# Copies and sums out of PSUM, split by bank, and an order that knows of the banks

## The chip, the cores and the metric

The kernel runs on one core of a Trainium2 chip. The metric is the device time of one execution in microseconds. Three timed runs of the kernel before gave 785.96, 789.14 and 790.19 us; the median, 789.14 us, is the time to compare with. A profiled execution of the same kernel had a span of 774.2 us from its first to its last instruction, with a granted TensorE clock of 0.997.

## The reference

Two blocks follow each other. The first is a linear recurrence over 768 positions, for 4 batches and 8 heads of width 40. The second sends each of the 3072 resulting rows (320 wide) to one of 8 experts, an expert being two matrix products with a ReLU between them.

```python
# r, k, v, w, a, b: (4, 8, 768, 40)
state = np.zeros((B, H, D, D), dtype=np.float32)
for t in range(S):
    kt, vt, rt = (k[:, :, t], v[:, :, t], r[:, :, t])
    wt, at, bt = (w[:, :, t], a[:, :, t], b[:, :, t])
    y[:, :, t] = np.einsum('bhd,bhde->bhe', rt, state)
    Sa = np.einsum('bhde,bhe->bhd', state, at)
    state_decay = state * wt[:, :, None, :] - np.einsum('bhd,bhe->bhde', Sa, bt)
    state = state_decay + np.einsum('bhd,bhe->bhde', vt, kt)

x = y.transpose(0, 2, 1, 3).reshape(B * S, H * D)          # (3072, 320)
logits = x @ w_gate                                        # 8 experts
expert_idx = np.argmax(logits, axis=1)
# gate_w: the softmax weight of the chosen expert
# for each expert e, over its rows:
h = np.maximum(x_sorted[lo:hi] @ w1[e], 0.0)               # w1[e]: 320 x 1024
y_sorted[lo:hi] = h @ w2[e]                                # w2[e]: 1024 x 320
# back in the order of the rows, times gate_w
```

## The kernel before

The recurrence is done in chunks of 64 positions. A **unit** is one chunk of half the batches; there are 24 (12 chunks, 2 halves). Inside a unit the effect of the 64 positions on each other is the inverse of a triangular matrix, which is built by repeated squaring: `X` holds a power, its transpose and a running sum, and three rounds double the power. Each round multiplies on TensorE into PSUM, and ScalarE and VectorE bring the products back to SBUF.

PSUM is one tile of 8 banks. A matmul group takes one bank or an even pair of them. In a pair the first index of the data (`q`, 0 or 1) is the bank, so bank 0 holds one half of the heads and bank 1 the other.

```python
psum = pp.tile([128, 8, 512], F32, name="ps")
def pair(h, width, w=0):                    # a pair of banks: x, bank, p, d
    return psum[:, h.at : h.at + 2, w * NP * C : w * NP * C + NP * width].rearrange("x a (p d) -> x a p d", p=NP)
def copy(e, dst, src):
    if e == ACT:
        nc.scalar.copy(dst, src)            # L494
    else:
        nc.vector.tensor_copy(dst, src)     # L496
def mm(out_, lhsT, rhs, start=True, stop=True):
    nc.tensor.matmul(...)                   # L499
```

Every operation of the recurrence is a `Step`: a rank, an engine (`ANY` is ScalarE or VectorE), a cost in us by the program's own model, a function that emits the instructions, and the `Held` objects that it reads and writes. `Held` stands for a piece of a buffer or for PSUM banks. Before anything is emitted, `in_order` walks over the steps that are ready, gives each a start on its engine, takes the one that can start first (the rank decides among equals) and emits it. The order of the instructions on each engine is the outcome. The semaphores that keep the engines apart are put in afterwards, by what each instruction reads and writes. For PSUM that is done by bank: two instructions of different engines on one bank follow each other in the order in which they were emitted, also where both only read.

```python
def when(s):
    return {e: max((d.done - (d.lag if d.on == e and e != SP else 0.0) for d in s.deps), default=0.0)
            for e in ((ACT, DVE) if s.eng == ANY else (s.eng,))}
# ...
for s, r in ready.items():
    new = [h for h in s.ps if h.at is None]
    for e in r:
        t0 = max(r[e], free[e])
        ask = t0 + (WAIT if s.eng == ANY and e == DVE else 0.0)     # WAIT = 1.00
        # ... free banks, cost
        key = (ask, s.rank[0] + uneven, s.rank, t0 + cost)
```

The model above lets two engines read one bank at a time.

The groups of matmuls whose result is read by two engines:

```python
# 1. N and GT out of one pair (p_a); the mask of GT is applied by GpSimd
Step(rk - 1.3, DVE, 0.69, ... nc.vector.tensor_tensor(d, s(), m, op=ALU.mult), reads=[ps], writes=held)      # N, L583
Step(rk - 2.0, ACT, 0.59, ... nc.scalar.copy(d, s()), reads=[ps], writes=held)                               # GT, L585
# 2. T and the first sums out of ONE bank (N transposed)
for i, (z, par) in enumerate(((0, 0), (1, 1), (0, 1), (1, 0))):
    Step(rk - 0.1, ANY, 0.36, ... copy(e, T1[halves[z], :, par, :], ...), reads=[ps], writes=hT1[i : i + 1])
Step(rk - 0.5, DVE, 1.38, first_sums, reads=[ps], writes=hX[2:3])                                            # L607
# 3. three squarings: new power, new transpose and new sum
def sums(e, dst, src, old):
    nc.vector.tensor_tensor(dst[:, 0], src[:, 0], old[:, 0], op=ALU.add)                                     # L620
    for h in range(2):
        o_ = halves[1 - h]
        nc.vector.tensor_tensor(dst[o_, 1], src[o_, 1], old[halves[h], 1], op=ALU.add)                       # L623
while 8 * k <= C:
    # a pair for the power: 16 matmuls, one copy
    Step(rk, PE, 4 * ROUND, ... p_power(e, pair(ps, C), X, 1, 0), reads=hX[:2], writes=[ps], n=64)
    Step(rk - 0.9, ANY, 0.59, ... copy(e, Xn[:, :, :, 0, :], pair(ps, C)), reads=[ps], writes=hXn[0:1])
    # a pair that holds both the transpose and the sum
    Step(rk, PE, 0.81, ... p_sum(e, half_sums(ps, 2), X, 2), reads=hX, writes=[ps], n=64)
    Step(rk, ANY, 0.59, ... copy(e, Xn[:, :, :, 1, :], half_sums(ps, 2)[:, :, :, 0, :]), reads=[ps], writes=hXn[1:2])
    Step(rk, DVE, 1.29, ... sums(e, Xn[:, :, :, 2, :], half_sums(ps, 2)[:, :, :, 1, :], X[:, :, :, 2, :]),
         reads=[ps] + hX[2:3], writes=hXn[2:3])
    X, hX = Xn, hXn
    k *= 2
# 4. M and TT out of the last pair
Step(rk, DVE, 0.69, ... nc.vector.tensor_tensor(M[:], half_sums(ps, 2)[:, :, :, 0, :], eye(2, NP), op=ALU.add), ...)   # M, L673
def kept(e, ps=ps, TT=TT):
    src = half_sums(ps, 2)[:, :, :, 1, :]
    copy(e, TT[:, 0], src[:, 0])
    for h in range(2):
        copy(e, TT[halves[h], 1], src[halves[1 - h], 1])
Step(rk + 0.1, ANY, 1.1, kept, reads=[ps], writes=hTT)
Step(rk - 1.0, POOL, 1.22, ... nc.gpsimd.tensor_tensor(TT[:], TT[:], X[:, :, :, 2, :], op=ALU.add), ...)               # L683
```

Further on a unit turns v and k (`nV`, `nKB`), adds the state (`rhs`, `W`, `Vu`, `ZU`), writes y and the new state, and computes the logits and the scaled rows `xs`. The first expert's work begins inside the same order; the others follow outside it.

Of the kernel before, what the change touches and what calls it, by code (L numbers as in the profile page):

```python
# [15 lines left out]
ALU = mybir.AluOpType  # L16
# [7 lines left out]
def kernel(  # L24
# [245 lines left out]

    class Step:
        def __init__(self, rank, eng, cost, fn, reads=(), writes=(), after=(), lag=0.2, n=0, shape=None, first=-1):
            self.rank, self.eng, self.cost, self.fn, self.lag, self.n = (rank, len(steps)), eng, cost, fn, lag, n
            self.shape, self.first = shape, shape if first == -1 else first
# [19 lines left out]
    def in_order():  # L294
# [13 lines left out]

        def place(new, t):

            ok = [f is not None and f <= t for f in bank_free]
            at = []
            for h in new:
                n = h.banks
                b = next((b for b in (range(7, -1, -1) if n == 1 else range(0, 8, 2)) if all(ok[b : b + n])), None)
                if b is None:
                    return None
                ok[b : b + n] = [False] * n
                at.append(b)
            return at  # L320
# [10 lines left out]
        while ready:  # L331
            times = sorted({f for f in bank_free if f is not None})
            best = None
            for s, r in ready.items():
                new = [h for h in s.ps if h.at is None]
                for e in r:
                    t0 = max(r[e], free[e])
# [45 lines left out]
            free[e] = end  # L383
            s.on, s.done = e, end + s.lag
            s.fn(e)
# [17 lines left out]
    with tc.tile_pool(name="ring", bufs=1) as ring, \  # L403
# [4 lines left out]
        class Ring:  # L408
# [19 lines left out]
        r_GT = Ring("GT", [NP, 2, C], 1)  # L428
        r_N = Ring("N", [NP, 2, C], 1)
        r_X = Ring("X", [2, NP, 3, C], 0)  # L430
        r_X.bufs = [
            (wx[:, i * XN : (i + 1) * XN].rearrange("x (q p w j) -> x q p w j", q=2, p=NP, w=3), [Held() for _ in range(3)]) for i in range(XB)
        ]
        r_M = Ring("M", [2, NP, C], 2)
        r_TT = Ring("TT", [2, NP, C], 2)
# [41 lines left out]
        for i, (name, cost, part) in enumerate(first_constants()):  # L477
            step = Step(-98.5 if name else -60 + i + 0.3, POOL, cost, lambda e, part=part: part(), writes=[h_ones] if name else [], lag=0.2)
            if not name:
                basis.append(step)  # L480
# [29 lines left out]
        def unit(u):  # L510
# [37 lines left out]
            Step(pre, DVE, 1.4, lambda e: nc.vector.tensor_tensor_scan(  # L548
# [3 lines left out]
            Step(pre, DVE, 0.2, lambda e: nc.vector.reciprocal(qi[:, :, 0], r3[:, :, 1]), reads=hrv, writes=hqi)  # L552
            Step(pre, ACT, 0.25, lambda e: nc.scalar.copy(pc[:], r3[:, :, 1]), reads=hrv, writes=hpc)
            Step(pre + 1.0, DVE, 1.3, lambda e: nc.vector.tensor_tensor_scan(  # L554
                qq[:], dec[:, : SEG * C1], qi[:].rearrange("p s j -> p (s j)"), 0.0, op0=ALU.mult, op1=ALU.add,
            ), reads=hdec + hqi, writes=hq)
            for q in range(2):
                kb = KB[:, :, q]
                by = behind[:, q * NP : (q + 1) * NP].unsqueeze(2).to_broadcast([128, NP, 2, C])
                Step(pre - 0.1, POOL, 1.2, lambda e, kb=kb, by=by: nc.gpsimd.tensor_tensor(kb, kb, by, op=ALU.mult),  # L560
                     reads=hrv + hKB[2:], writes=hKB[q : q + 1])
            Step(pre, POOL, 1.22, lambda e: nc.gpsimd.tensor_tensor(Aq[:], Aq[:], q3[:, :, :C], op=ALU.mult), reads=hq, writes=hA)  # L562
# [12 lines left out]
            Step(rk - 1.0, PE, 0.81, p_a, reads=hKB + hA, writes=[ps], n=64)  # L575
            for t, held, i, mask, by in ((N1, hN1, 1, m_neg, DVE), (GT, hGT, 0, m_low, ACT)):
# [5 lines left out]
                if by == DVE:  # L582
                    Step(rk - 1.3, DVE, 0.69, lambda e, d=dst_, s=src_, m=mask: nc.vector.tensor_tensor(d, s(), m, op=ALU.mult), reads=[ps], writes=held)  # L583
                else:
                    Step(rk - 2.0, ACT, 0.59, lambda e, d=dst_, s=src_: nc.scalar.copy(d, s()), reads=[ps], writes=held)  # L585
                    Step(rk, POOL, 1.2, lambda e, d=dst_, m=mask: nc.gpsimd.tensor_tensor(d, d, m, op=ALU.mult), writes=held)  # L586
# [11 lines left out]
            Step(rk - 0.6, PE, 0.47, by_blocks(N1, ps), reads=hN1, writes=[ps], n=8, shape=WHOLE)  # L598
            blocks = lambda ps=ps: psum[:, ps.at, :].rearrange("x (p z j) -> x p z j", p=NP, z=2)
            for i, (z, par) in enumerate(((0, 0), (1, 1), (0, 1), (1, 0))):  # L600
                Step(rk - 0.1, ANY, 0.36, lambda e, z=z, par=par, blocks=blocks: copy(e, T1[halves[z], :, par, :], blocks()[halves[par], :, z, :]),
                     reads=[ps], writes=hT1[i : i + 1])
# [8 lines left out]
            Step(rk - 0.5, DVE, 1.38, first_sums, reads=[ps], writes=hX[2:3])  # L611
            Gk, hGk = r_Gk.take()
            ps = Held(1)
            Step(rk - 0.6, PE, 0.47, by_blocks(GT, ps), reads=hGT, writes=[ps], n=8, shape=WHOLE)
            Step(rk + 1.0, ANY, 0.59, lambda e, ps=ps: copy(e, Gk[:].rearrange("x p z j -> x (p z j)"), psum[:, ps.at, :]), reads=[ps], writes=hGk)
# [3 lines left out]
            def sums(e, dst, src, old):  # L619
                nc.vector.tensor_tensor(dst[:, 0], src[:, 0], old[:, 0], op=ALU.add)  # L620
                for h in range(2):
                    o_ = halves[1 - h]
                    nc.vector.tensor_tensor(dst[o_, 1], src[o_, 1], old[halves[h], 1], op=ALU.add)  # L623
# [9 lines left out]
            for i in range(2):  # L633
                Step(rk, ANY, 0.59, lambda e, i=i, ps=ps, X=X: copy(e, X[:, :, :, i, :], pair(ps, C, i)), reads=[ps], writes=hX[i : i + 1])
# [17 lines left out]
            while 8 * k <= C:  # L652
# [3 lines left out]
                Step(rk, PE, 4 * ROUND, lambda e, ps=ps, X=X: p_power(e, pair(ps, C), X, 1, 0), reads=hX[:2], writes=[ps], n=64)  # L656
                Step(rk - 0.9, ANY, 0.59, lambda e, ps=ps, Xn=Xn: copy(e, Xn[:, :, :, 0, :], pair(ps, C)), reads=[ps], writes=hXn[0:1])
                ps = Held(2)
                Step(rk, PE, 0.81, lambda e, ps=ps, X=X: p_sum(e, half_sums(ps, 2), X, 2), reads=hX, writes=[ps], n=64)
                Step(rk, ANY, 0.59, lambda e, ps=ps, Xn=Xn: copy(e, Xn[:, :, :, 1, :], half_sums(ps, 2)[:, :, :, 0, :]),  # L660
                     reads=[ps], writes=hXn[1:2])
                Step(rk, DVE, 1.29, lambda e, ps=ps, X=X, Xn=Xn: sums(
                    e, Xn[:, :, :, 2, :], half_sums(ps, 2)[:, :, :, 1, :], X[:, :, :, 2, :],
                ), reads=[ps] + hX[2:3], writes=hXn[2:3])
# [6 lines left out]
            Step(rk, PE, 0.81, lambda e, ps=ps, X=X: p_sum(e, half_sums(ps, 2), X, 2), reads=hX, writes=[ps], n=64)  # L671

            Step(rk, DVE, 0.69, lambda e, ps=ps, M=M: nc.vector.tensor_tensor(  # L673
                M[:], half_sums(ps, 2)[:, :, :, 0, :], eye(2, NP), op=ALU.add,
            ), reads=[ps], writes=hM)

            def kept(e, ps=ps, TT=TT):
                src = half_sums(ps, 2)[:, :, :, 1, :]
                copy(e, TT[:, 0], src[:, 0])
                for h in range(2):  # L680
                    copy(e, TT[halves[h], 1], src[halves[1 - h], 1])
            Step(rk + 0.1, ANY, 1.1, kept, reads=[ps], writes=hTT)
            Step(rk - 1.0, POOL, 1.22, lambda e, X=X, TT=TT: nc.gpsimd.tensor_tensor(TT[:], TT[:], X[:, :, :, 2, :], op=ALU.add), reads=hX[2:3], writes=hTT)  # L683

# [5 lines left out]
            Step(rk - 0.1, ANY, 0.59, lambda e, ps=ps: copy(e, nV[:].rearrange("x p a d -> x (p a d)"), psum[:, ps.at, :]), reads=[ps], writes=hnV)  # L690
# [11 lines left out]
            for i in range(2):  # L702
                Step(rk + 0.4, ANY, 0.59, lambda e, i=i, ps=ps: copy(
                    e, nKB[:, i * NP : (i + 1) * NP].rearrange("x b a d -> x (b a d)"), psum[:, ps.at + i, :],
                ), reads=[ps], writes=hnKB[i : i + 1])
# [25 lines left out]
            Step(rk - 0.1, PE, 8 * ROUND if c else 4 * ROUND, p_rhs, reads=hGk + hnV + (hST + hA if c else []), writes=[ps], n=128 if c else 64)  # L731
# [6 lines left out]
            Step(rk + 3.7, ANY, 0.85, to_rhs, reads=[ps], writes=hrhs)  # L738
# [9 lines left out]
            Step(rk + 0.7, PE, 4 * ROUND, p_w, reads=hM + hrhs, writes=[ps], n=64)  # L748
            Step(rk + 0.3, ANY, 0.42, lambda e, ps=ps: copy(e, W[:, :, :, :D], pair(ps, D)), reads=[ps], writes=hW)
            if c:  # L750
                ps = Held(1)
                Step(rk, PE, 0.47, by_blocks(ST, ps), reads=hST, writes=[ps], n=8, shape=WHOLE)
                Step(rk, ANY, 0.42, lambda e, ps=ps: copy(
# [13 lines left out]
            Step(rk + 0.1, PE, 4 * ROUND, p_uT, reads=hTT + hW, writes=[ps], n=64)  # L767
# [22 lines left out]
            for s in range(2):  # L790
                Step(rk + 0.5, DVE, 0.69, lambda e, s=s, ps=ps: nc.vector.tensor_tensor(
                    ZU[:, s, :, :C], psum[:, ps.at + s, :].rearrange("x (b j) -> x b j", j=C),
                    m_plus[:, None, :].to_broadcast([128, SEG, C]), op=ALU.mult,
                ), reads=[ps], writes=hZU[s : s + 1])
            if not last:
                ps = Held(2)
                Step(rk + 0.3, PE, 0.92, turned(lambda p, par: Vu[:, p, 2 * par : 2 * par + 2], ps), reads=hV + huT, writes=[ps], n=16, shape=WHOLE)
                for i in range(2):
# [3 lines left out]
                    Step(rk + 0.4, ANY, 0.42, uv, reads=[ps], writes=hZU[2 + i : 3 + i])  # L802
# [14 lines left out]
            Step(rk + 0.4, PE, (0.57 if c else 0) + 0.48 + 0.96 * w / 104, p_y, reads=hnKB + (hZU[:2] if last else hZU) + (hSn + hR if c else []), writes=[psy], n=128 if c else 64, shape=TALL, first=None if c else TALL)  # L817
# [22 lines left out]
            Step(late, PE, 1.0, p_x, reads=hxT + [h_tg], writes=[psx], n=16, shape=WHOLE)  # L840
# [10 lines left out]
            Step(late + 0.6, DVE, 0.4, logits, reads=[psx], writes=[hl])  # L851
            Step(late + 0.3, ACT, 0.5, lambda e: nc.scalar.activation(
# [468 lines left out]
```

## Time and profile before

| what | value |
|---|---|
| median of three runs | 789.14 us |
| span of the profiled execution | 774.2 us |
| ScalarE: 128x512 copies into wx | 192 of 590 ns |
| VectorE: sums of a squaring, L620 (128x256) and L623 (64x256) | 72 and 144 of 422 ns |
| VectorE: first sums, L607 (64x512) | 48 of 688 ns |
| GpSimd: GT's mask, L586 | 24 of 1310 ns |
| DMA | 61.06 MB, mean 79 GB/s |

How to read it: PE is TensorE's matmul row and PEld its weight-load row, DVE is VectorE, ACT ScalarE, POOL GpSimd. Lines such as L494 are lines of the kernel; because every copy goes through one helper, the tile names (`wx<-ps`) tell the operations apart. `wx` is the buffer of the powers `X`. Two stages are seen in the span: the recurrence to about 505 us, with many small matmuls (64 x 64), and the experts after it, with few large ones.

### The profile page before, as it was taken

What the parts mean: (1) busy time and instruction counts of PE and PEld (TensorE: products, weight loads), DVE (VectorE), ACT (ScalarE), POOL (GpSimd) and SP (SyncE); (2) the same over time, 40 slices, a digit from 0 to 9 for tenths busy, and PEclk for the clock granted to TensorE, in tenths of its full rate; (3) what the DMA queues carried; (4) which work ended last, traced back from release to release, by engine and by line L of the source; (5) the groups of instructions that cost most, each with busy time, mean ns of one, the idle gap of its engine ahead of it and who ended that gap; (6) DMA issues with size and microseconds to landing.
All of it is one profiled execution on the core that took longest, in us unless ns stands there. A gap on an engine that the chain in (4) does not pass through costs nothing. (4 is left out here: it accounts for less than half of the span.)

```text
span 774.2 us, 35470 instructions
## 1 busy us (share of the span) xinstructions
PE 715.5 (92%) x15712; PEld 554.2 (72%) x15712; DVE 371.9 (48%) x804; ACT 346.9 (45%) x840; POOL 291.8 (38%) x472
## 2 busy tenths in 40 slices
PE   3988999999998998999999898799999999999995
PEld 2877888888877887888988888665656565564653
DVE  7667666667666666667576666640201112010110
ACT  2665766566665665666757666421101111111010
POOL 8742145723653366334852470313413110111101
PEclk9999999999999999999999999999999999999998
DMA  4332223323212321232232211333953126002000
GB/s 96 87 79 56 66 59 72 98 53 93 64 40 70 81 68 41 71 97 74 65 77 71 52 31 41 112 92 117 330 161 130 51 78 207 23 16 84 24 0 28
DMA packets 120368, 61.06 MB, mean 79 GB/s; under 512 B 100688, under 2 KB 116051, under 8 KB 120212
## 3 DMA queue, kind: packets, MB, share of 16 engines
q1 hardware_dynamic: 112776, 46.20, 22.5%
q0 software_dynamic: 3136, 9.44, 3.7%
q10 hardware_dynamic: 4300, 3.12, 1.4%
q8 instruction: 124, 2.03, 1.1%
q14 instruction: 32, 0.26, 0.1%
HBM read 50.08 MB, written 9.31 MB: 77 GB/s over the span
## 5 line engine op out<-in xcount | busy, mean ns | idle before, releaser
L499 PE MATMUL ps<-wx 64*64 64x128 f32 (+1 forms) x5376 | 147.4, 251 | 11.6 <-ACT wx L494 7.6
L494 ACT COPY wx<-ps 128x512 f32<-128x512 f32 (+1 forms) x196 | 110.8, 587 | 79.1 <-PE ps L499 42.6
L499 PEld LDWEIGHTS ps<-wx 64*64 64x64 f32 x5376 | 124.2, 134 | 25.4 <-ACT wx L494 10.8
L1160 DVE TENSOR_SCALAR h_sb<-hp 128x448 f32<-128x448 f32 (+1 forms) x32 | 18.4, 574 | 189.1 <-PE hp L1155 162.6
L247 POOL DMA_INDIRECT out_dram<-zo,s_idx x21 | 20.8, 989 | 150.2 <-ACT zo L1177 149.6
L1171 PE MATMUL zp<-w,h_sb 128*128 128x320 f32 (+1 forms) x272 | 71.0, 433 | 0.0
L560 POOL TENSOR_TENSOR KB<-KB,rv 128x512 f32<-128x512 f32 x48 | 58.3, 1235 | 18.0 <-DMA KB<-in_packed_dram 5.7
L623 DVE TENSOR_TENSOR wx<-ps,wx 64x256 f32<-64x256 f32 x144 | 60.8, 422 | 3.0
L1161 ACT ACTIVATE h_sb<-hp 128x448 f32<-128x448 f32 (+1 forms) x32 | 16.1, 504 | 101.2 <-PE hp L1155 52.0
L1171 PEld LDWEIGHTS zp<-w,h_sb 128*128 128x128 f32 (+1 forms) x272 | 44.4, 174 | 20.5 <-issue 1.3
L1177 ACT COPY zo<-zp 128x320 f32<-128x320 f32 x25 | 10.7, 426 | 104.9 <-PE zp L1171 104.9
L562 POOL TENSOR_TENSOR A<-A,q 128x512 f32<-128x512 f32 x24 | 28.4, 1185 | 72.9 <-DVE q L554 55.0
L620 DVE TENSOR_TENSOR wx<-ps,wx 128x256 f32<-128x256 f32 x72 | 30.4, 422 | 53.1 <-ACT wx L494 32.5
L586 POOL TENSOR_TENSOR GT<-GT,m_low 128x512 f32<-128x512 f32 x24 | 31.4, 1310 | 61.6 <-ACT GT L585 61.6
L683 POOL TENSOR_TENSOR TT<-TT,wx 128x512 f32<-128x512 f32 x24 | 30.8, 1281 | 62.4 <-ACT TT L494 61.8
L1171 PE MATMUL zp<-wx,h_sb 128*128 128x320 f32 (+1 forms) x192 | 53.0, 433 | 0.0
L1147 PE MATMUL hp<-xgT,w 128*128 128x448 f32 x128 | 51.1, 547 | 0.0
L494 ACT COPY T<-ps 64x256 f32<-64x256 f32 x94 | 34.5, 367 | 35.6 <-DVE wx L607 29.3
L1171 PEld LDWEIGHTS zp<-wx,h_sb 128*128 128x128 f32 (+1 forms) x192 | 33.4, 177 | 13.2 <-issue 0.8
L1147 PEld LDWEIGHTS hp<-xgT,w 128*128 128x128 f32 x128 | 23.5, 190 | 25.8 <-issue 25.5
L499 PE MATMUL ps<-ZU,nKB 128*64 128x104 f32 (+1 forms) x768 | 38.8, 253 | 0.1
L607 DVE TENSOR_TENSOR wx<-ps,ihalf 64x512 f32<-64x512 f32 x48 | 33.0, 688 | 8.1 <-ACT T L494 2.1
(246 smaller groups left out, 1362.2 us busy)
## 6 DMA issues: line engine op xcount, KB each, us to landing
KB<-in_packed_dram SPq DMA_DIRECT2D x188, 40.0 KB
w<-in_moe_w_dram SPq DMA_DIRECT2D x16, 320.0 KB
x_rows<-xs SPq DMA_DIRECT2D x24, 192.0 KB
w<-in_moe_w_dram SPq DMA_DIRECT2D x8, 512.0 KB
dec<-in_packed_dram SPq DMA_DIRECT2D x96, 40.0 KB
Vu<-in_packed_dram SPq DMA_DIRECT2D x96, 40.0 KB
wx<-in_moe_w_dram SPq DMA_DIRECT2D x12, 320.0 KB
A<-in_packed_dram SPq DMA_DIRECT2D x92, 40.0 KB
```

Of the source, the lines that this page charges most:

```text
L247: ins_ = nc.gpsimd.indirect_dma_start(out=out[:, :], out_offset=bass.IndirectOffsetOnAxis(ap=si, axis=0), in_=zo, in_offset=None, bounds_c ...
L494: nc.scalar.copy(dst, src)
L499: nc.tensor.matmul(out_, lhsT=lhsT, rhs=rhs, start=start, stop=stop, skip_group_check=True)
L560: Step(pre - 0.1, POOL, 1.2, lambda e, kb=kb, by=by: nc.gpsimd.tensor_tensor(kb, kb, by, op=ALU.mult), reads=hrv + hKB[2:], writes=hKB[q : ...
L562: Step(pre, POOL, 1.22, lambda e: nc.gpsimd.tensor_tensor(Aq[:], Aq[:], q3[:, :, :C], op=ALU.mult), reads=hq, writes=hA)
L586: Step(rk, POOL, 1.2, lambda e, d=dst_, m=mask: nc.gpsimd.tensor_tensor(d, d, m, op=ALU.mult), writes=held)
L607: nc.vector.tensor_tensor(for_q[:, :, ::-1] if par else for_q, blocks()[halves[par]], ihalf[halves[par], None, None, :].to_broadcast([HP, ...
L620: nc.vector.tensor_tensor(dst[:, 0], src[:, 0], old[:, 0], op=ALU.add)
L623: nc.vector.tensor_tensor(dst[o_, 1], src[o_, 1], old[halves[h], 1], op=ALU.add)
L683: Step(rk - 1.0, POOL, 1.22, lambda e, X=X, TT=TT: nc.gpsimd.tensor_tensor(TT[:], TT[:], X[:, :, :, 2, :], op=ALU.add), reads=hX[2:3], wri ...
L1147: nc.tensor.matmul(hps[i][:, : c1 - c0], lhsT=w[0][:, db, (fb + i) * 128 : (fb + i + 1) * 128], rhs=xT[:, db, c0:c1], start=(db == 0 and n ...
L1171: nc.tensor.matmul(zp[r0 : r0 + n], lhsT=h[:, fb, c0 : c0 + n], rhs=w[2][:, fb, :], start=(fb == 0), stop=(fb == FB - 1), skip_group_check ...
```

## The change

Where two engines read a pair of banks, each reading is split into one for each bank, and the two engines begin with different banks: ScalarE with bank 1, VectorE with bank 0. The pieces of `X`, `N`, `GT`, `M` and `TT` get a `Held` for each bank. A `Step` may name the bank that it reads (`bank=`), and the model keeps for each bank the last step that touched it, so that a step of another engine starts after it. Nothing is changed in the matmuls or in what is computed. Many ranks were set anew with it.

```diff
     class Held:
         def __init__(self, banks=0):
             self.last, self.readers, self.banks, self.at, self.users = None, [], banks, None, 0
+            self.seen = [None] * banks
...
+        def behind(s, e):
+            if e == PE:
+                return []
+            return [d for h in s.ps for d in (h.seen if s.bank is None else h.seen[s.bank : s.bank + 1]) if d is not None and d.on != e]
...
-                    t0 = max(r[e], free[e])
+                    t0 = max(r[e], free[e], *(d.done for d in behind(s, e)))
...
+            s.deps.update(behind(s, e))
             s.on, s.done = e, end + s.lag
+            if e != PE:
+                for h in s.ps:
+                    for b in range(h.banks) if s.bank is None else (s.bank,):
+                        h.seen[b] = s
...
# N and GT
+                for b in range(2) if by == DVE else (1, 0):
+                    if by == DVE:
+                        Step(rk, DVE, 0.42, ... nc.vector.tensor_tensor(d[:, b], s()[:, b], m[:, b], op=ALU.mult), ..., bank=b)
+                    else:
+                        Step(rk - 1.0, ACT, 0.36, ... nc.scalar.copy(d[:, b], s()[:, b]), ..., bank=b)
...
# T and the first sums: still one bank, other ranks
-                Step(rk - 0.1, ANY, 0.36, ... copy(e, T1[halves[z], :, par, :], ...
+                Step(rk + 0.3, ANY, 0.36, ... copy(e, T1[halves[z], :, par, :], ...
-            Step(rk - 0.5, DVE, 1.38, first_sums, reads=[ps], writes=hX[2:3])
+            Step(rk - 0.6, DVE, 1.38, first_sums, reads=[ps], writes=hX[3:])
...
# the squarings
-                Step(rk, ANY, 0.59, ... copy(e, Xn[:, :, :, 1, :], half_sums(ps, 2)[:, :, :, 0, :]), reads=[ps], writes=hXn[1:2])
-                Step(rk, DVE, 1.29, ... sums(...), reads=[ps] + hX[2:3], writes=hXn[2:3])
+                for q in (1, 0):
+                    Step(rk, ANY, 0.36, ... copy(e, Xn[:, q, :, 1, :], half_sums(ps, 2)[:, q, :, 0, :]),
+                         reads=[ps], writes=hXn[1 + q : 2 + q], bank=q)
+                for q in range(2):
+                    Step(rk + 1.0, DVE, 0.84 if q else 0.42, ... sums(e, q, ...),
+                         reads=[ps] + hX[3 + q : 4 + q], writes=hXn[3 + q : 4 + q], bank=q)
...
# M and TT
-            Step(rk, DVE, 0.69, ... M[:] ...)
+            for q in range(2):
+                Step(rk - 0.1, DVE, 0.42, ... M[:, q] ..., bank=q)
-            Step(rk + 0.1, ANY, 1.1, kept, reads=[ps], writes=hTT)
+            for q in (1, 0):
+                Step(rk - 0.4, ANY, 0.72 if q else 0.36, kept, reads=[ps], writes=hTT[q : q + 1], bank=q)
...
# readings that were already one bank each now say so (nKB, ZU, xs, the first expert's ReLU), for instance
-                Step(rk + 0.5, DVE, 0.69, ... ZU ..., reads=[ps], writes=hZU[s : s + 1])
+                Step(rk, DVE, 0.69, ... ZU ..., reads=[ps], writes=hZU[s : s + 1], bank=s)
...
# some of the other ranks
-            Step(rk - 1.0, PE, 0.81, p_a, ...)
+            Step(rk, PE, 0.81, p_a, ...)
-            Step(rk + 3.7, ANY, 0.85, to_rhs, reads=[ps], writes=hrhs)
+            Step(rk + 0.3, ANY, 0.85, to_rhs, reads=[ps], writes=hrhs)
```

## The prediction

> **What bounds the kernel now.** I read, in this order: the busy shares of the page, the windows (how the span divides into stages), the waits of the weight-load row inside the first stage, the waits of ScalarE and VectorE there, the groups by shape (what one instruction costs), and last the timeline of one unit. The page's busy line:
>
> ```profile
> PE 715.5 (92%) x15712; PEld 554.2 (72%) x15712; DVE 371.9 (48%) x804; ACT 346.9 (45%) x840; POOL 291.8 (38%) x472
> ```
>
> TensorE is the fullest engine, but that is a mean over two stages. In the windows each row is a stretch, its length, then busy time and instruction count of PE, PEld, DVE, ACT, POOL, clock, DMA share, GB/s:
>
> ```profile
> 200.00:300.00 100.00, 93.04 (x3042) 81.96 (x3038) 66.13 (x129) 63.34 (x156) 53.07 (x106) 1.00 0.27 64
> ...
> 600.00:700.00 100.00, 100.00 (x380) 57.53 (x380) 13.28 (x25) 11.22 (x23) 12.84 (x13) 1.00 0.21 73
> ```
>
> From about 505 us to the end (269 us of the span, the experts) PE has no idle time and the other engines are nearly empty. The change's splits do not live there, so I take that stage as unchanged. From 20 to 505 us (the recurrence, 24 units, so 485 / 24 = 20.2 us a unit) PE is 7% idle, the weight-load row 18%, and VectorE and ScalarE work two thirds of the time. What the stage can give back is what TensorE waits there. The weight-load row shows it best, because a matmul's modelled end runs into the next gap. Its waits from 20 to 505 us (total us, times, longest):
>
> ```profile
> PEld ps L499 <- issue: 20.8, 87, 2.0
> PEld ps L499 <- ACT wx L494: 14.0, 21, 2.2
> ...
> PEld ps L499 <- ACT T L494: 3.6, 11, 0.8
> PEld ps L499 <- DVE M L673: 3.5, 6, 0.8
> ...
> PEld ps L499 <- ACT nV L494: 3.0, 3, 1.5
> ```
>
> All rows of that answer whose releaser is ACT add up to about 36 us, those of DVE to 7.5 us, "issue" rows (nothing the profile shows[...]) to 29 us, the rest 3 us. So **about 43 us of 485 are waits for the two engines that empty PSUM**, and no change to those engines can return more than that. The two engines in turn wait for each other in the same stretch:
>
> ```profile
> ACT T L494 <- DVE wx L607: 27.6, 21, 1.9
> ACT wx L494 <- DVE wx L623: 21.0, 15, 2.6
> ...
> ACT TT L494 <- DVE M L673: 6.3, 10, 0.9
> ```
>
> ```profile
> DVE wx L620 <- ACT wx L494: 32.5, 38, 2.2
> ...
> DVE N L583 <- ACT GT L585: 12.0, 11, 1.5
> ...
> DVE M L673 <- ACT TT L494: 6.3, 9, 1.4
> ```
>
> None of these six is a use of the other's result: both read one matmul's output out of the same banks (the copy wx L494 against the sums wx L620 and L623, N against GT, M against TT, T against the first sums L607). Together they are 27.6 + 21.0 + 6.3 + 32.5 + 12.0 + 6.3 = 105.7 us of waiting. The timeline shows how one gets to TensorE:
>
> ```profile
> 268.96 1.39 DVE L607 TENSOR_TENSOR wx<-ps,ihalf 64x512 f32<-64x512 f32 x2
> ...
> 270.44 0.36 ACT L494 COPY T<-ps 64x256 f32<-64x256 f32 x1 [1.51 <-DVE wx L607]
> 270.83 0.59 ACT L494 COPY nV<-ps 128x512 f32<-128x512 f32 x1
> ...
> 271.46 0.69 PE L499 MATMUL ps<-R,S 64*64 64x64 f32 x30 [1.15 <-ACT nV L494]
> ```
>
> ScalarE's copy of T waits 1.51 us for VectorE to leave the bank, the copy of nV stands behind it, and PE stands 1.15 us for nV, although nV had nothing to do with that bank. The order was made by a model that did not know of the first wait.
>
> [...]
>
> **The change part by part.** The cost of a split, from the groups by shape (after the bar: busy us, mean ns):
>
> ```profile
> L494 ACT COPY wx<-ps 128x512 f32<-128x512 f32 x192 | 108.9, 590 | 77.2 <-PE ps L499 42.6 <-DVE wx L623 21.0 <-PE ps L697 3.1
> ...
> L673 DVE TENSOR_TENSOR M<-ps,ihalf 128x512 f32<-128x512 f32 x24 | 16.5, 686 | 10.0 <-ACT TT L494 6.3 <-PE ps L499 3.6
> ```
>
> The half size is 373 ns on ScalarE (TT, 128x256) and 422 ns on VectorE (L620, 128x256). Two halves cost 2 × 373 - 590 = 156 ns more on ScalarE and 2 × 422 - 686 = 158 ns more on VectorE.
>
> *Added.* Per unit: GT one copy more, each of three squarings one copy more (4 × 156 ns = 0.62 us, nearly all on ScalarE, which took 192 of 192 such copies), N and M one operation more each (2 × 158 ns = 0.32 us on VectorE). The sums (three operations per squaring) and TT (three copies) keep their count. Over 24 units that is 15.0 us on ScalarE and 7.6 us on VectorE: their shares rise from about 64 and 66% to 67 and 68%. Neither becomes the bound on average.
>
> *Removed: the serial reading of a pair of banks.* Squaring: copy 0.590 and then sums 3 × 0.422 = 1.266, serial 1.86 us plus a handover; after it ScalarE takes bank 1 (0.373) while VectorE takes bank 0 (0.422), then they swap, and VectorE's 1.27 us is the longer side: about 0.6 us less, three times a unit. M and TT: 0.686 + 3 × 0.373 = 1.81 serial; crossed, about 1.2: 0.6 less. N and GT: 0.69 + 0.59 = 1.28 against about 0.85: 0.4 less. Together 3 × 0.6 + 0.6 + 0.4 = 2.8 us a unit by which PSUM pairs come free and operands arrive earlier, 67 us over 24 units. Most of it lies beside other matmuls, because TensorE works on another unit or branch meanwhile; only what stands in the 43 us can come back.
>
> *What comes back.* Of the 43 us, rows that name the split groups (wx, M, GT, TT over all PE rows) are about 25 us (wx 14.0 + 3.0 + 1.0 + 0.5, M 3.5, GT 1.0 + 0.3, TT 0.9 + 0.8). The wx row mixes split copies (three of eight per unit) with copies of the squares and powers that are still whole but stand behind them in ScalarE's queue; and a copy's own time stays. I choose half: **12.5 us**. The other 18 us (T, nV, Vu, ZU, rhs and so on) are not split, but the new model knows that readers of a bank follow each other, and should put nV ahead of a T copy that cannot start. I choose a third: **6 us**. Against that the 15 us more in the queue that most often releases PE: I choose a quarter, **4 us**. Net 12.5 + 6 - 4 = 14.5 us: 789.1 - 14.5 = **775 us** (the profiled span is 774.2 us and the timed median 789.1; I carry the difference in us over), a 1.8% gain. Matmul count, expert stage and "issue" waits I leave as they are. The many changed ranks reorder everything; I give them no gain of their own and widen the range.
>
> **The rivals.** (a) *Hidden anyway.* TensorE is fed from another branch while a pair is drained; then the mutual waits vanish and PE's waits only change names, or go to "issue" (29 us, which nothing here touches). For it: 106 us of mutual waits come with only 43 us of PE waits. It would leave 784 to 790 us. (b) *ScalarE becomes the one waited for.* Its queue gets 96 instructions more, and ACT already releases five sixths of the 43 us. If its share of PE waits grows by half, +15 us: about 800 us. Against it: a third of its time is free and it loses up to 33 us of waits on the split groups. (c) *The order decides.* A truer model could take away most of the head-of-line waits, 30 us of 43: 759 us. [...]
>
> **Range and chances.** The floor is 789 - 43 = 746 if every such wait went. Half of that, 22 us, would be a good result (767); 30 us an excellent one. So 757 to 792 should hold it 8 times in 10. Two per cent is 15.8 us, so the line is at 773.4, just below my number: faster by over 2% 0.45, within 2% 0.46, slower by over 2% 0.09.
>
> **What the changed profile would show.** Right: the rows of ACT for DVE L623, DVE L620 for ACT, N for GT and M for TT shrink from 78 us (21.0 + 32.5 + 12.0 + 6.3 + 6.3) to below 30; 120 whole wx copies of 590 ns and 144 half copies near 373 ns in place of 192 whole ones; PEld's waits for ACT wx fall from 14 to about 7 us; the recurrence stage ends near 490 instead of 505 us, and the experts still take 269 us. Wrong: mutual waits gone but the stage as long as before (a); ACT busy over 70% and more PE waits for it (b); wait rows of T for L607 gone while those of the split groups stay (c). A change in the expert stage of more than 5 us would be outside this account.

## The result, and the profile after

Four timed runs of the changed kernel gave 763.01 to 765.93 us, median 764.25 us; four of the kernel before on the same chip gave 785.96 to 790.19 us, median 787.76 us. The ratio is **0.9701 (95% interval 0.9665 to 0.9737)**: 23.5 us or 3.0% faster. The prediction had 775 us and a range of 757 to 792.

The busy line of the page after:

```profile
PE 720.6 (94%) x15712; PEld 558.6 (73%) x15712; DVE 375.3 (49%) x844; ACT 356.3 (47%) x944; POOL 296.1 (39%) x472
```

PE and PEld have the same number of instructions as before. ScalarE has 104 more and VectorE 40 more, and ScalarE's busy time is up by 356.3 - 346.9 = 9.4 us. So the engines that empty PSUM do more work in a shorter span. The same two windows as before (stretch, length, then PE, PEld, DVE, ACT, POOL, clock, DMA share, GB/s):

```profile
200.00:300.00 100.00, 97.99 (x3273) 87.01 (x3268) 70.12 (x150) 69.56 (x190) 59.95 (x108) 1.00 0.30 72
...
600.00:700.00 100.00, 100.00 (x388) 56.83 (x387) 13.67 (x26) 11.19 (x23) 10.80 (x11) 1.00 0.24 82
```

In this stretch of 100 us TensorE gets through 3273 matmuls where it did 3042, 7.6% more, and its idle time fell from 7 us to 2. Over the whole recurrence the change is smaller: PE was busy for 449.8 of 487 us before (92.4%) and for 451.6 of 470 after (96.1%). The expert window is as full as it was. What the weight-load row waits for from 20 to 490 us (total us, times, longest):

```profile
PEld ps L513 <- issue: 23.9, 98, 3.1
...
PEld ps L513 <- ACT wx L508: 3.7, 20, 0.4
...
PEld ps L513 <- ACT T L508: 0.8, 2, 0.6
...
PEld ps L513 <- DVE M L692: 0.5, 1, 0.5
```

The lines have moved: the helper's copy is now line 508 and its matmul 513, the first sums are line 624, the sums of a squaring line 639, N line 598 and M line 692. The wait for copies into `wx` kept its count (20 for 21) but its longest fell from 2.2 to 0.4 us: the long ones are gone. The row for `nV` (3.0 us before) is gone. The mutual waits of ScalarE and of VectorE, in the same stretch:

```profile
ACT T L508 <- DVE wx L624: 10.0, 13, 1.5
...
ACT wx L508 <- DVE wx L639: 1.1, 3, 0.4
...
ACT TT L508 <- DVE M L692: 0.4, 1, 0.4
```

```profile
DVE wx L639 <- ACT wx L508: 5.5, 7, 2.2
...
DVE M L692 <- ACT TT L508: 3.6, 11, 0.7
...
DVE N L598 <- ACT GT L601: 0.5, 1, 0.5
```

The crossed pairs hardly wait for each other. What is left is mainly T behind the first sums, which read a single bank and can't be crossed. The cost of one instruction, by shape:

```profile
L508 ACT COPY wx<-ps 128x512 f32<-128x512 f32 x120 | 68.9, 591 | 25.8 <-PE ps L513 22.9 <-ACT nKB L508 0.7 <-DVE q L568 0.5
...
L508 ACT COPY wx<-ps 128x256 f32<-128x256 f32 x144 | 52.0, 376 | 41.7 <-PE ps L513 38.7 <-DVE wx L639 1.1 <-ACT wx L508 0.5
...
L692 DVE TENSOR_TENSOR M<-ps,ihalf 128x256 f32<-128x256 f32 x48 | 20.1, 422 | 14.3 <-PE ps L513 8.8 <-ACT TT L508 3.6 <-ACT g L871 0.9
```

Before, the idle time ahead of the `wx` copies named VectorE with 21.0 us; now nearly all of it names PE, the matmul whose product is to be copied.

**Where the time went.** The recurrence (to the last matmul for the logits) ended at 507.1 us and now ends at 489.5, 17.6 us earlier. From there to the first expert matmul it is 25.4 us instead of 26.4. The experts, from their first matmul to the end, took 240.7 us before and 249.3 after. So the two spans, 774.2 and 764.2 us, differ by 17.6 + 1.0 - 8.6 = 10.0 us only, while the timed medians differ by 23.5. The 8.6 us need a cause of their own; they are taken up with the third group of runs.

### The profile page after: what moved, and what is told of

Its sections match the earlier page's. It is cut to its first block, busy times and chain, and to the rows that moved or that the text cites. A ratio compares the mean times of both kernels' runs of the same rounds, so it can differ in the third digit from the quotient of the medians.

```text
span 764.2 us, 35640 instructions
## 1 busy us (share of the span) xinstructions
PE 720.6 (94%) x15712; PEld 558.6 (73%) x15712; DVE 375.3 (49%) x844; ACT 356.3 (47%) x944; POOL 296.1 (39%) x472
## 4 chain that ended last, share of the span: by engine, by line
PE 49%; issue 29%; POOL 11%; DMA 3%; DVE 3%; SPq 2%; ACT 1%; POOLq 0%; DVEq 0%; ACTq 0%
PE ps L513 39%; PE ps L608 5%; PE ps L716 5%; POOL out_dram L247 3%; POOL xg L1144 2%; SPq L545 2%; DMA dec<-in_packed_dram 1%; POOL oh_r L990 1%; POOL oh_c L991 1%; DVE rv L562 1%; POOL A L576 1%; DVE wx L639 1%; ACT wx L508 1%; POOL TT L702 0%; POOL KB L574 0%
## 5 line engine op out<-in xcount | busy, mean ns | idle before, releaser
L513 PE MATMUL ps<-wx 64*64 64x128 f32 (+1 forms) x5376 | 152.4, 253 | 2.0 <-issue 0.9
L508 ACT COPY wx<-ps 128x512 f32<-128x512 f32 (+2 forms) x268 | 119.9, 474 | 70.3 <-PE ps L513 61.6
L513 PEld LDWEIGHTS ps<-wx 64*64 64x64 f32 x5376 | 127.2, 134 | 17.9 <-issue 6.7
L639 DVE TENSOR_TENSOR wx<-ps,wx 64x256 f32<-64x256 f32 (+1 forms) x216 | 91.2, 422 | 36.5 <-PE ps L513 22.6
L574 POOL TENSOR_TENSOR KB<-KB,rv 128x512 f32<-128x512 f32 x48 | 56.8, 1200 | 47.0 <-DMA KB<-in_packed_dram 14.5
L1196 ACT COPY zo<-zp 128x320 f32<-128x320 f32 x25 | 10.6, 425 | 106.6 <-PE zp L1190 102.7
L1190 PEld LDWEIGHTS zp<-w,h_sb 128*128 128x128 f32 (+1 forms) x272 | 44.4, 174 | 20.5 <-issue 1.3
L810 DVE TENSOR_TENSOR ZU<-ps,m_plus 128x512 f32<-128x512 f32 x48 | 30.9, 686 | 27.6 <-PE ps L513 27.5
L702 POOL TENSOR_TENSOR TT<-TT,wx 128x512 f32<-128x512 f32 x24 | 32.5, 1356 | 30.1 <-ACT TT L508 25.2
L1166 PEld LDWEIGHTS hp<-xgT,w 128*128 128x128 f32 x128 | 23.5, 190 | 25.8 <-issue 25.5
L562 DVE TENSOR_TENSOR_SCAN rv<-dec,ones 128x521 f32<-128x521 f32 x24 | 37.2, 1551 | 10.5 <-DMA dec<-in_packed_dram 5.6
```

Of the source, the lines that this page charges most:

```text
L513: nc.tensor.matmul(out_, lhsT=lhsT, rhs=rhs, start=start, stop=stop, skip_group_check=True)
L562: Step(pre - 0.1, DVE, 1.4, lambda e: nc.vector.tensor_tensor_scan(rv[:, : SEG * C1 + 1][:, ::-1], dec[:, ::-1], ones65[:, ::-1], 0.0, op0 ...
L574: Step(pre + 0.6, POOL, 1.2, lambda e, kb=kb, by=by: nc.gpsimd.tensor_tensor(kb, kb, by, op=ALU.mult), reads=hrv + hKB[2:], writes=hKB[q : ...
L639: nc.vector.tensor_tensor(dst[o_, q], src[o_, q], old[o, q], op=ALU.add)
L702: Step(rk - 0.1, POOL, 1.22, lambda e, X=X, TT=TT: nc.gpsimd.tensor_tensor(TT[:], TT[:], X[:, :, :, 2, :], op=ALU.add), reads=hX[3:], writ ...
L1166: nc.tensor.matmul(hps[i][:, : c1 - c0], lhsT=w[0][:, db, (fb + i) * 128 : (fb + i + 1) * 128], rhs=xT[:, db, c0:c1], start=(db == 0 and n ...
```

## The experiments

Two theories, and a rival. **Crossing**: two engines no longer stand in each other's way at a pair of banks, so operands come earlier and banks free up earlier; the split itself gives the gain. **Order**: what counts is that the order is made with knowledge of who can't read when, so that other work is emitted meanwhile; the split is only what the order was planned with. The rival is that the **ranks**, set anew in the same change, give the gain. The change is thus three: split (S), model (M), ranks (R). All kernels below compute everything. Times are set against the kernel before, timed beside them on the same chip, because that kernel took 788 us in the result above and on the chip of the first group, and 778 us on the two chips of the other groups. The expectations name times for a kernel before of 788 us; in the second and third group their distance from it is what can be compared.

### First group: one part undone, and the order held fixed

**merged**: the changed kernel with its order of steps, but where two halves of a reading stood, the first emits nothing and the second emits the whole. The matmuls' order is that of the changed kernel.

```diff
-    Step(rk, ANY, 0.36, ... copy(e, Xn[:, q, :, 1, :], half_sums(ps, 2)[:, q, :, 0, :]), ..., bank=q)
+    Step(rk, ANY, 0.36, ... both(Xn, lambda e: copy(e, Xn[:, :, :, 1, :], half_sums(ps, 2)[:, :, :, 0, :]), e, (ps, 1)), ..., bank=q)
# both(): does nothing at the first call with a key, calls the function at the second;
# the same for N, GT, the sums, M and TT
```

> The changed kernel with its order kept: each engine takes the same steps in the same order, but the two halves of N, GT, the squarings' copies and sums, M and TT are emitted as one whole where the second half stood. Theory A (the split itself, two engines on two banks, is the gain): most of the 23.5 us comes back, 780 to 790 us, and the waits of L620/L639 for ACT and of ACT for the sums return to over 60 us. Rival B (the order made by a model that knows of the banks is the gain): 764 to 772 us.

Measured: 771.47 us, ratio 0.9758 (0.9696 to 0.9820), as B had it. Most of the gain (2.4 of 3.0%) stays without any split reading. The interval reaches over that of the change itself, so the size of the split's own part is left to a second run below.

**no_split**: model and new ranks, readings whole and planned as whole.

```diff
-    for q in (1, 0):
-        Step(rk, ANY, 0.36, ... copy(e, Xn[:, q, :, 1, :], ...), ..., bank=q)
+    Step(rk, ANY, 0.59, ... copy(e, Xn[:, :, :, 1, :], ...), reads=[ps], writes=hXn[1:3])
# sums, N, GT, M and TT likewise
```

> The model that knows of the banks and the new ranks, no split anywhere, the order made anew for that. A: 780 to 790 us. B: at most 772 us, since the model can now plan around the serial readings.

Measured: 786.66 us, ratio 0.9983 (0.9962 to 1.0004): no gain, as A had it. The window over its recurrence:

```profile
20.00:509.00 489.00, 457.58 (x14622) 404.90 (x14623) 306.65 (x650) 313.14 (x766) 228.39 (x384) 0.97 0.28 70
```

The mean clock is 0.97 (the figure ahead of the DMA share); in the changed kernel it is 0.99 from 20 to 490 us. Its trace has three stretches of 3.4 us with a granted clock of 0.50, together 10.2 us; in no_split such stretches at half clock add up to 30.7 us of the recurrence, by estimate worth up to 15 us (half of it). So part of this loss may be clock. It does not tell how much the missing split costs the plan.

**no_model**: split and new ranks, and the model lets two engines read one bank at a time, as before.

```diff
         def behind(s, e):
-            if e == PE:
+            if True:
                 return []
```

> Split and new ranks, but the model lets two engines read one bank at a time as before. A: 764 to 771 us. B: 778 to 790 us, with the waits of ACT T for the first sums back near 27 us.

Measured: 786.69 us, ratio 0.9966 (0.9946 to 0.9986): almost no gain, with 17.1 us at half clock (mean clock 0.98 from 20 to 510 us). What it lost shows in ScalarE's row for T:

```profile
ACT T L508 <- DVE wx L624: 25.4, 20, 1.7
```

25.4 us, where the changed kernel has 10.0, as B had foretold: the blind model again puts the copies of T ahead of what could run.

**old_ranks**: split and model, with the ranks of the kernel before.

```diff
-            Step(rk, PE, 0.81, p_a, ...)
+            Step(rk - 1.0, PE, 0.81, p_a, ...)
# and all other ranks as before the change
```

> Split and model as in the change, all ranks as before. A and B: 764 to 771 us. Rival C (the newly set ranks are the gain): 778 to 790 us.

Measured: 771.86 us, ratio 0.9778 (0.9733 to 0.9824). Split and model alone bring three quarters of the gain (2.2 of 3.0%). The ranks as its main source (C) fall away.

### Second group: one part alone

On another chip, with the kernel before profiled again.

**before_again**: no edit.

> The kernel before once more, for a second profile: the first one had a span of 774 us where the timed runs took 788, and a granted clock of 1.000 in the recurrence where the changed kernel's profile shows several stretches of 3.4 us at half clock. If the missing 12 us are clock, this profile has a span near 786 us, with more stretches at half clock and the same waits; if they are waits, PEld's gaps grow by about 12 us at the same clock.

Measured: 776.56 us, span 774.8 us, recurrence to 507.7 us. Mutual waits, PEld's waits for ScalarE and VectorE (43.4 us) and the groups repeat the first profile within 1 us. So neither of the two expectations came: the kernel takes 776 us here, like the execution first profiled (776.0 us), and 777.9 us as the median of eleven timed runs on this chip. The first profile stands beside these, and not beside the timed runs of 786 to 790 us.

**split_only**: split readings, the old ranks, the blind model (the line of no_model).

```diff
-                Step(rk, ANY, 0.59, ... copy(e, Xn[:, :, :, 1, :], ...
+                for q in (1, 0):
+                    Step(rk, ANY, 0.36, ... copy(e, Xn[:, q, :, 1, :], ...
```

> The split alone: ranks and blind model of the kernel before. A (the split is the gain): 768 to 775 us. B (a model that knows of the banks is needed as well, as no_model suggests): 782 to 790 us.

**model_only**: the model, the old ranks, whole readings.

```diff
-                    t0 = max(r[e], free[e])
+                    t0 = max(r[e], free[e], *(d.done for d in behind(s, e)))
```

> The model alone: ranks of before, no split. A: 785 to 790 us. B in its strong form (the order alone is the gain): at most 775 us. If no_split's 787 us were bad luck of its ranks, this one should be well below it.

**ranks_only**: the new ranks (with them the planned cost of GT's mask, 1.3 for 1.2 us) and nothing else.

```diff
-            Step(rk - 1.0, PE, 0.81, p_a, ...)
+            Step(rk, PE, 0.81, p_a, ...)
# and all other ranks as in the change
```

> The new ranks alone: blind model, no split. C (the ranks are the gain): at most 780 us. A and B: 785 us or more.

Measured, with the first group and the change, all against the kernel before:

| kernel | parts | median, us | ratio (95% interval) | mutual waits, us: split groups / T with first sums |
|---|---|---|---|---|
| before_again | none | 776.56 (one execution) | 1 | 85.7 / 29.6 |
| split_only | S | 769.39 | 0.9896 (0.9879 to 0.9914) | 31.4 / 24.6 |
| model_only | M | 768.94 | 0.9912 (0.9885 to 0.9939) | 42.4 / 2.2 |
| ranks_only | R | 784.56 | 1.0094 (1.0066 to 1.0122) | 81.7 / 29.5 |
| old_ranks | S M | 771.86 | 0.9778 (0.9733 to 0.9824) | 13.4 / 7.8 |
| no_model | S R | 786.69 | 0.9966 (0.9946 to 0.9986) | 36.4 / 29.3 |
| no_split | M R | 786.66 | 0.9983 (0.9962 to 1.0004) | 47.3 / 6.5 |
| the change | S M R | 764.25 | 0.9701 (0.9665 to 0.9737) | 13.0 / 12.8 (after_again) |

The mutual waits are sums of the rows of ScalarE and VectorE that name each other's readings of these groups, over 20 to 490 us. They show two parts that do two different things. The split takes down the first figure (85.7 to 31.4) and leaves T at 24.6; the model takes T down (29.6 to 2.2), where nothing is split, and halves the first figure too (42.4). The two rows of each, split_only and then model_only (its first sums are line 622, its sums line 637):

```profile
ACT T L508 <- DVE wx L624: 22.5, 18, 2.2
...
DVE wx L639 <- ACT wx L508: 4.4, 9, 1.0
```

```profile
DVE wx L637 <- ACT wx L508: 16.0, 23, 2.6
...
ACT T L508 <- DVE wx L622: 0.5, 2, 0.3
```

Each brings about 1% (9 us), between what the two theories expected of it, and both together 2.2%, about what the two add up to (1.9%). The ranks cost 0.9% alone, as both theories had it, cost 0.7% with the split and 0.7% with the model, and gain 0.8% with both. They belong to the order that the other two make, and carried to another they harm. Part of these differences may be clock: no_split ran 30.7 us of its recurrence at half clock and model_only 6.8 (mean clocks 0.97 and 0.99), by estimate up to 12 us of time (half of the difference), so the 0.7% with the model can be that alone. Likewise old_ranks had 20.5 us and the change 10.2 (mean clocks 0.98 and 0.99), up to 5.1 us of the 7.6 us between them. The intervals of old_ranks and the change also touch, so the 0.8% is the least sure of these.

### Third group: the same order, three ways to read a pair

**after_again**: the changed kernel, no edit, on a third chip.

> The changed kernel on the chip of the next three, as their base. Its ratio to before should be 0.97 whatever the chip: 764 us where before takes 788, about 755 where before takes 778. If the ratio falls to 0.98, a part of the first 23.5 us belonged to that chip's clock in the expert stage and not to the change.

Measured: 755.05 us (753.58 to 758.16) against 777.7 for the kernel before, ratio 0.9701 (0.9678 to 0.9725). The gain is the same 3.0% where both kernels are faster.

This run also settles the experts' 8.6 us. The windows over the experts, before_again and then after_again:

```profile
534.00:774.00 240.00, 232.26 (x911) 133.96 (x911) 29.46 (x56) 26.82 (x58) 45.54 (x47) 0.99 0.30 99
```

```profile
515.00:756.00 241.00, 232.26 (x911) 133.94 (x911) 29.45 (x56) 27.30 (x60) 45.66 (x47) 0.99 0.30 98
```

PE 232.26 us in both: the stage is the same, 240.7 and 240.8 us from its first matmul. In the first profile of the changed kernel, PE stood still for 3.5 us at 532 us, and this followed (first the window of the stop, then the one after it):

```profile
532.00:536.00 4.00, 0.45 (x7) 0.31 (x5) 0.00 (x0) 0.54 (x1) 2.83 (x3) 0.94 1.05 302
536.00:550.00 14.00, 13.99 (x62) 11.92 (x63) 3.01 (x9) 0.89 (x4) 0.00 (x0) 0.65 0.50 163
```

A mean clock of 0.65 over 14 us is (1 - 0.65) × 14 / 0.5 = 9.8 us at half speed (0.50 from 535.6 to 545.7 us), by estimate 4.9 us of time. The busy time of PE agrees: 237.15 us for the 911 matmuls from 515 us to the end, against 232.26 in after_again, 4.9 us more. With the stop of 3.5 us it makes 8.4 of the 8.6. after_again has neither: its clock is 1.00 in the same two windows, and PE is busy for all of both. All four profiles of the first group, on a chip where the kernel before took 788 us, have an expert stage of 248.8 to 250.3 us; the profiles from the two others have about 240.7. The kernel before, as first profiled, has 240.7 too and a device time 10 us or more below its timed runs, so it is to be set beside those others. The change is not the cause of the 8.6 us. Why PE stops there in the first profile is not settled: the trace names nothing ("issue").

**same_bank**: the changed kernel and its order, but ScalarE too begins with bank 0. Split, not crossed.

```diff
-    ... lambda e, ps=ps, Xn=Xn, q=q: copy(e, Xn[:, q, :, 1, :], half_sums(ps, 2)[:, q, :, 0, :]),
+    ... lambda e, ps=ps, Xn=Xn, q=1 - q: copy(e, Xn[:, q, :, 1, :], half_sums(ps, 2)[:, q, :, 0, :]),
# GT (b=1 - b) and TT (q=1 - q) likewise
```

> The changed kernel, its order kept, with the same number and size of copies; only that ScalarE takes its two halves of GT, of the squarings' copies and of TT in the other order, so that both engines begin with bank 0. If the gain of the split is that two engines work on two banks, one engine now waits about 0.4 us per pair, five pairs a unit: half or more of the loss of the merged kernel, 3 to 6 us over the changed kernel, and the waits between ScalarE and VectorE grow. If only earlier freed halves matter, less than 2 us.

Measured: 761.03 us, ratio 0.9794 (0.9756 to 0.9833): 6 us slower than after_again, at the upper end of what was expected. Its mutual waits in the split groups are 98.8 us, after_again's 13.0.

**merged_2**: merged once more, on this chip.

```diff
# the edit of merged
```

> The merged kernel again (the changed kernel's order, whole readings), on the same chip as the changed kernel. Its first runs lay between 763 and 773 us. From its trace, where the recurrence ends 6.8 us later than in the changed kernel: 6 to 8 us over the changed kernel.

Measured: 758.11 us (756.39 to 760.78), ratio 0.9741 (0.9718 to 0.9763): 3.1 us slower than after_again, where 6 to 8 were expected; the two intervals touch. What the two engines wait for each other in it (after_again has 13.0 us in all split groups):

```profile
ACT wx L508 <- DVE wx L652: 25.9, 36, 3.4
DVE wx L652 <- ACT wx L508: 24.4, 23, 4.6
DVE M L705 <- ACT TT L508: 21.7, 18, 2.7
```

The 3.1 us are not taken at one clock. In its recurrence merged_2 ran 6.8 us at half clock and after_again 13.7, by estimate worth up to 3.4 us (half of the difference); over all timed runs the mean clocks are 0.995 and 0.991. (The two profiles of the changed kernel have 10.2 and 13.7 us, so this figure varies by itself.) The first profiles of merged and of the changed kernel both have 10.2 us at half clock; there merged was 7.2 us slower, its recurrence 6.7 us longer. So the split's own part, with the order held, is 3.1 us as timed here and an estimated 6 to 7 us at an equal clock. About that also reaches PEld: its waits for ScalarE and VectorE are 27.9 us in merged_2 and 20.8 in after_again.

One squaring in the three timelines (start, us, engine, line), the changed kernel first, then same_bank, then merged_2:

```profile
260.22 1.10 PE L513 MATMUL ps<-wx 64*64 64x128 f32 x32
...
261.41 1.31 DVE L639 TENSOR_TENSOR wx<-ps,wx 128x256 f32<-128x256 f32 x3
261.41 0.83 ACT L508 COPY wx<-ps 128x256 f32<-128x256 f32 x2 [1.06 <-PE ps L513]
...
262.16 1.19 PE L513 MATMUL ps<-turn_gate,xT 128*128 128x136 f32 x8
...
263.29 0.33 PE L513 MATMUL ps<-wx 64*64 64x64 f32 x6
```

```profile
262.90 0.37 ACT L508 COPY wx<-ps 128x256 f32<-128x256 f32 x1 [1.00 <-PE ps L513]
...
263.30 1.31 DVE L639 TENSOR_TENSOR wx<-ps,wx 128x256 f32<-128x256 f32 x3 [0.34 <-ACT wx L508]
...
264.70 0.37 ACT L508 COPY wx<-ps 128x256 f32<-128x256 f32 x1 [1.43 <-DVE wx L639]
```

```profile
261.95 1.30 DVE L652 TENSOR_TENSOR wx<-ps,wx 128x256 f32<-128x256 f32 x3
...
263.34 0.59 ACT L508 COPY wx<-ps 128x512 f32<-128x512 f32 x1 [2.44 <-DVE wx L652]
```

Crossed, both engines begin at 261.41 and the pair is empty 1.31 us later. Begun at the same bank, three turns follow each other: 262.90 to 265.07, 2.17 us. Whole: 261.95 to 263.93, 1.98 us. So the crossing saves 0.7 to 0.9 us here, as step "Removed" of the prediction had it (0.6). But in the changed kernel PE does not take the next power when the operands are there: it works on the logits (`turn_gate`) until 263.35. The order has put other matmuls under the reading, and here the time saved is hidden. This one squaring fits with the whole: merged_2 has 79.4 us of mutual waits in its split groups against 13.0, and of these 66 us more only 7.1 reach PEld.

**search_b**: the changed kernel with many ranks moved, found by a search for an earlier end in the program's own model (3 us earlier there).

```diff
-            Step(rk, PE, 0.81, p_a, ...)
+            Step(-0.2 + rk, PE, 0.81, p_a, ...)
-            Step(pre - 0.1, DVE, 1.4, ... rv ...)
+            Step(-1.5 + pre - 0.1, DVE, 1.4, ... rv ...)
# and many others
```

> The changed kernel with ranks moved by a search that minimised the end that the program's own model gives the order (3 us less than with the ranks of the change). If the model with banks is true to a few us, 1 to 4 us under the changed kernel; if the model's last microseconds are noise, within 5 us of it on either side.

Measured: 754.74 us (752.27 to 756.74), ratio 0.9707 (0.9682 to 0.9731), the same as after_again: the second of the two expectations. 3 us by the model are not to be seen in the time. No version is clearly faster than the changed kernel.

## Why the prediction was right, and which terms were off

The waits that the prediction named are the ones that fell, and the time fell in the range; the gain was 23.5 us instead of 14.5. What it had wrong is how much of this each part of the change brings. The working was a sum of three terms over PEld's waits for ScalarE and VectorE, so it can be taken term by term. The same rows added up over the recurrence, before and after (20 to 505 and 20 to 490 us):

| rows of PEld | before | after | predicted back | measured back |
|---|---|---|---|---|
| ACT and DVE, split groups (wx, N, GT, M, TT) | 25.5 | 9.8 | 12.5 | 15.7 |
| ACT and DVE, all others (T, nV, Vu, ZU, rhs ...) | 18.4 | 10.6 | 6 | 7.8 |
| charge for ScalarE's longer queue | | | -4 | not seen |
| sum | 43.9 | 20.4 | 14.5 | 23.5 |
| "issue" | 28.6 | 31.2 | 0 | -2.6 |
| GpSimd and DMA | 3.3 | 4.8 | 0 | -1.5 |

- **The term "I choose half" for the split groups was mis-sized:** 15.7 of 25.5 us came back, three fifths. The term also put all of this down to the split. With the order held, merged_2 has 18.5 us in these rows and after_again 11.4, so the crossing takes 7.1 us away and the order about as much (before_again has 25.0).
- **The third for the others was close:** 7.8 of 18.4 us. The reason given, nV no longer behind a T copy, is seen: T's mutual wait went from 27.6 to 10.0 us and the nV row of PEld is gone. In model_only, with the old ranks and nothing split, T's mutual wait is 2.2 us and PEld has no nV row either, so the model alone is enough for it.
- **The charge of 4 us for ScalarE's queue was wrong.** The instructions cost what was worked out (376 ns for a half, 591 for a whole; 144 and 120 of them): ScalarE's copies of `wx` and GT add up to 138.2 us where they were 123.0, 15.2 us more. Its busy row, in which overlapping records count once, rose by 9.4. But PE waits less for ScalarE, not more (36.2 us before, 15.8 after). The work more went, it seems, into the third of the time in which that queue stood idle; no run measured this apart, so a cost that the other two rows hide can't be ruled out. In this sum it is the largest single error: 4 of the 9 us.
- **"I give the ranks no gain of their own"**: alone they cost 0.9%, so that was right for them by themselves; with split and model they go with some 0.8%, about 6 us, of which up to 5 can be clock.
- **What the profile was to show.** The five mutual rows went from 78 to 1.1 + 5.5 + 0.5 + 3.6 + 0.4 = 11 us (foretold: below 30); PEld's row for `wx` from 14 to 3.7 us (7); the recurrence ended at 489.5 us (490). The experts kept their length on the chips that can be compared.
- **The carried difference of span and median was not a constant.** I carried 15 us from the span (774.2) to the median (789.1). After, span and median agree (764.2 and 764.25): that profile has the stop and the half clock in the experts, and the profile before had not. The difference of the two first profiles, 10.0 us, would have misled; the ratio to runs on the same chip came out as 0.9701 on both chips where it was taken.

Of the rivals, (a) hidden anyway: wrong for the whole, since 23.5 us came back, but right for most of the mutual waits that the split removes in the changed order, as merged_2 shows. (b) ScalarE becomes the one waited for: wrong, its rows shrank. (c) The order decides: right for the larger part. With the order fixed, 19.6 of 22.7 us remain without a single split reading on one chip (777.7 - 758.1 of 777.7 - 755.05) and 2.4 of 3.0% in the first group. But the truer model alone, which this rival put at 759 us, brought only 9 us.

So the split gave a good part of its gain in a way that the prediction didn't see. Besides the 3 to 7 us that the crossing saves, it works as a thing to plan with: an order planned with halves that cross is a good order even for whole readings (merged_2, 0.974), while an order planned with whole readings under the same model is worth less (model_only 0.991, no_split 0.998). **What stays open** is why: in no_split up to 15 us may be half clock, and with two sets of ranks, one of them fitted to the change, it can't be said whether the halves make better orders as such or whether this is one lucky order. Many sets of ranks with and without halves would tell; that was not tried. The waits of PEld also don't account for the end to the last microsecond. 23.5 - 2.6 - 1.5 = 19.4 us less waiting and an estimated 5.1 us lost to half clock (half of 10.2) should have brought the recurrence 14.3 us forward; it came 17.6.

## What to carry to other kernels

When a fixed order of instructions comes out of a model, first put into the model what really keeps engines apart: here one rule, that readers of a bank follow each other (ScalarE's copies of T waited 27.6 us for VectorE's first sums in the kernel before), was worth as much alone (0.9%) as the split alone (1.0%). Measure what of a wait reaches the engine that sets the end before removing it: 66 us of mutual waits were worth 3 to 7 us when the order already had work beneath them. Undo each part of a change alone and together, since a tuning fitted to the rest (the ranks) is a loss without it.

## What the runs showed of the hardware

- **Half a reading cost more than half.** A 128x256 reading of PSUM took 376 ns on ScalarE (whole 591) and 422 ns on VectorE (whole 686): 161 and 158 ns for each further instruction. Splitting without crossing pays this and showed no gain here: same_bank is 2.9 us slower than merged_2, though their intervals touch.
- **The clock stood at one half in stretches of 3.4 us.** In the recurrence of the changed kernel's first trace there are three, from 20.1, 139.6 and 470.7 us, each 3.4 us long with a granted clock of 0.50; between them it is 1.00. A window ahead of the second, and the window that holds it:

```profile
136.00:139.00 3.00, 0.63 (x24) 0.66 (x28) 2.93 (x6) 0.78 (x3) 0.88 (x2) 1.00 0.00 0
139.50:143.00 3.50, 3.50 (x72) 3.17 (x76) 0.76 (x2) 2.29 (x8) 0.00 (x0) 0.51 0.46 124
```

  In the 3.4 us just ahead of the three, PE was busy for 1.48, 1.23 and 2.09 us. A stretch as empty was not always followed by half clock: in the recurrence of the kernel before, as first profiled, the clock is 1.00 from 20 to 505 us, and there PE was busy for 1.09 of 3.4 us at one place (301.5 to 304.9 us) and 1.58 at another (241.2 to 244.6). So what brings the half clock on is not shown by these traces. In the second profile of the kernel before, 6.8 us of the recurrence are at half clock (mean clock 0.99). The stretches in one recurrence add up to 6.8, 10.2, 13.7, 17.1, 20.5 or 30.7 us (mean clocks 0.99 to 0.97), 2 to 9 times 3.4. By estimate each 3.4 us at half clock cost up to 1.7 us, half its length; among the experts 9.8 us of it went with 4.9 us more of PE's busy time.
- **One kernel took different times on different chips.** The kernel before took 788 us on one and 778 on two others, each at one time; the merged kernel took 771.47 us where it took 788, and 758.11 on one of the others. In the traces of the changed kernel the experts' stage alone is 249.3 us on the first and 240.8 on the other.
